# Weights' decode: VectorE's five operations with one tensor input get a column of constants as a second tensor input

## The chip, the core and the metric

The kernel runs on one core of one Trainium2 chip. The metric is the device time of one execution in microseconds (us); less is better. Before the change it is 2730.36 us, the median of three runs.

## What is computed

Three layers follow each other on 2 x 12480 tokens with 128 features: a long convolution with a filter that a small network makes of the positions, done by Fourier transforms and gated by x; a layer 128 to 2048 to 128 with a squared ReLU; and a layer 128 to 2048 to 128 with h cos(h).

```python
def _attn_ref(x, v, pos_emb, w1, w2):
    h_mlp = np.maximum(pos_emb @ w1, 0.0) @ w2
    h_filt = h_mlp * np.exp(-0.01 * pos)[:, None]
    u = x * v
    Uf = np.fft.rfft(u, n=2 * S, axis=1)
    Hf = np.fft.rfft(h_filt, n=2 * S, axis=0)
    y = np.fft.irfft(Uf * Hf[None], n=2 * S, axis=1)[:, :S]
    return x * y

def _moe_ref(x, w_in, w_out):
    h = x @ w_in
    r = np.maximum(h, 0.0)
    return (r * r) @ w_out

def _moe2_ref(x, w_in, w_out):
    h = x @ w_in
    return (h * np.cos(h)) @ w_out
```

The four weight matrices are drawn in double precision. The kernel gets their bits as pairs of 32-bit integers and splits each weight into a high and a low part, for matmuls in three terms.

## The kernel before

The work has three stages. The **first stage** takes the first transform of the convolution in 30 chunks of two pairs each (the loop over `n, (q, i)`). A pair multiplies x by v on GpSimd (L191), takes the filter's small network through TensorE and ScalarE (L182 to L198), runs eight matmul records into A (L212), copies one half to SBUF on ScalarE (L214) and adds and subtracts on VectorE into bt (L216), which is then stored to HBM. Loads of chunks come from the SP queue into five buffers, and a load is issued when TensorE has freed its buffer; bt has three buffers. The **second stage** (from about 230 us) takes the second transform, multiplies the spectra and goes back. The **third stage** (from about 470 us) runs the last transform and the two layers as one long loop of matmuls with operations of ScalarE, VectorE and GpSimd between them.

The change lies in the **decode of the weights**, the generator `weight(step)`. It has sixteen steps, one for each quarter of each matrix (four of sixteen row or column blocks, so 128 x 512 elements). A step reads `raw` in SBUF, whose pairs of integers give `lo` and `hi`, and works on the tiles w_a, w_b and w_r: VectorE masks the sign away (L102), takes the sign and sets a bit of it (L103), bounds the magnitude (L105), shifts the exponent into place (L107), puts sign and magnitude together (L108), takes the power of two alone (L110), and multiplies the low half by it (L113). ScalarE rounds to the high part wh (L112), and GpSimd makes the low part wl in two operations (L115, L117). All of these tiles lie in SBUF.

The generator is cut into seven pieces by its `yield`s. The first stage's loop takes two pieces behind each pair with `decode(2)`, from the third pair on, so that a step is spread over three and a half pairs and the sixteen steps over 56 of the 60. The order on each engine is the order in which the program issues: VectorE runs the decode's pieces between the bt of the pairs, and GpSimd runs L115 and L117 between the L191, which are issued four pairs ahead. Where L115 waits for L113, the L191 behind it wait as well.

Of the kernel before, what the change touches and what calls it, by code (L numbers as in the profile page):

```python
# [8 lines left out]
F32 = mybir.dt.float32  # L9
F32R = mybir.dt.float32r  # L10
I32 = mybir.dt.int32
U32 = mybir.dt.uint32
AF = mybir.ActivationFunctionType
ALU = mybir.AluOpType
# [43 lines left out]
def conv_moe(ctx, tc, t):  # L58
    nc = tc.nc
    cst = ctx.enter_context(tc.tile_pool(name="cst", bufs=1))  # L60
# [4 lines left out]
    nc.vector.memset(halfpi, HALF_PI)  # L65
    quarter = cst.tile([128, 1], F32, name="quarter")
    nc.vector.memset(quarter, -0.25)
    warm = cst.tile([128, 1], F32, name="warm")
    Gt = cst.tile([2 * HB, 2, 128], F32, name="Gt")
    It = cst.tile([128, 2, 2 * HB], F32, name="It")  # L70
# [10 lines left out]
    def raw_of(step):  # L81
        m, f0 = divmod(step, 4)
        f = slice(4 * f0, 4 * f0 + 4)
        raw = wt.tile([128, 4, 128, 2], I32, tag="wr", name="wr", bufs=2)
        src = t[("moe_w_in", "moe_w_out", "moe2_w_in", "moe2_w_out")[m]].bitcast(I32)
        src = src.rearrange("(f p) (e t) -> p f e t" if m % 2 else "p (f e t) -> p f e t", f=NF, t=2)
        nc.sync.dma_start(out=raw, in_=src[:, f])
        raws[step] = raw, W[1 + m // 2, m % 2], f

    def weight(step):  # L90
        if step not in raws:
            raw_of(step)
        n = WORDER.index(step) + 1
        if n < 16:
            raw_of(WORDER[n])
        raw, (wh, wl), f = raws.pop(step)
        lo, hi = raw.bitcast(U32)[:, :, :, 0], raw[:, :, :, 1]
        a, b, r = (wt.tile([128, 4, 128], I32, tag=f"w_{n}", name=f"w_{n}") for n in "abr")
        af, bf, rf = a.bitcast(F32), b.bitcast(F32), r.bitcast(F32)
        ts = nc.vector.tensor_scalar  # L100
        yield
        ts(out=a, in0=hi, scalar1=0x7fffffff, scalar2=None, op0=ALU.bitwise_and)  # L102
        ts(out=b, in0=hi, scalar1=-0x80000000, scalar2=0x40000000, op0=ALU.bitwise_and, op1=ALU.bitwise_xor)  # L103
        yield
        ts(out=af, in0=af, scalar1=2.0 ** -15, scalar2=122880.0, op0=ALU.max, op1=ALU.min)  # L105
        yield
        ts(out=a, in0=a, scalar1=4, scalar2=1, op0=ALU.logical_shift_left, op1=ALU.logical_shift_right)  # L107
        nc.vector.tensor_tensor(out=a, in0=a, in1=b, op=ALU.bitwise_xor)  # L108
        yield
        ts(out=b, in0=a, scalar1=-0x800000, scalar2=None, op0=ALU.bitwise_and)  # L110
        yield
        nc.scalar.activation(wh[:, f], af, AF.Copy)  # L112
        nc.vector.scalar_tensor_tensor(out=rf, in0=lo, scalar=2.0 ** -52, in1=bf, op0=ALU.mult, op1=ALU.mult)  # L113
        yield
        nc.gpsimd.tensor_tensor(out=bf, in0=af, in1=wh[:, f].bitcast(F32), op=ALU.subtract)  # L115
        yield
        nc.gpsimd.tensor_tensor(out=wl[:, f], in0=bf, in1=rf, op=ALU.add)  # L117

    steps = (x for k in WORDER for x in weight(k))

    def decode(n):
# [683 lines left out]
```

## Time and profile before

| | us |
|---|---|
| median of three runs | 2730.36 |
| lowest, highest | 2729.28, 2736.08 |
| the profiled execution | 2726.36 |
| its span, first to last instruction | 2724.3 |

The profiled execution is the one that the profile was taken of. Its rows are times from the span's start. PE is TensorE (PEld its weight loads), DVE VectorE, ACT ScalarE, POOL GpSimd, SP SyncE, whose queue issues most transfers; an engine's name with a q is its sequencer. L12 is line 12 of the kernel. An instruction's duration counts what it waits inside, once it has been started; what an engine waits for a semaphore before it stands apart, as idle time with the one that ended it.

### The profile page before, as it was taken

The page shows a single profiled execution, that of the slowest core. Times are in us where ns is not written, and L with a number is a line of the kernel's source. Part 1 is how long each engine was busy: PE and PEld are TensorE (multiplying, and loading weights), DVE is VectorE, ACT ScalarE, POOL GpSimd, SP SyncE. Part 2 cuts the span into 40 slices and gives each one's busy share as a digit, 9 for nine tenths or more (in the row PEclk, how much of TensorE's full clock was granted, in tenths as well). Part 3 has the DMA queues.
Part 4 walks back from the last instruction along what each step waited for, and adds up shares of the span by engine and source line. Part 5 has one row for each costly group of instructions (what it writes and reads, how often), then busy time and mean ns, then how long its engine had stood idle before and what let it go on. Part 6 is the DMA issues. An engine that isn't in the chain of part 4 may idle for free.

```text
span 2724.3 us, 38773 instructions
## 1 busy us (share of the span) xinstructions
PE 2681.8 (98%) x11762; PEld 2104.9 (77%) x11762; DVE 2402.7 (88%) x4675; ACT 2383.1 (87%) x4295; POOL 1353.2 (50%) x1050
## 2 busy tenths in 40 slices
PE   8998999999999999999999999999999999999999
PEld 5554444888888888888888888888888888888887
DVE  6997998888888888888888888888888888888888
ACT  4446997899999999999999999999999999999998
POOL 4565886244444444444444444444444444444455
PEclk9999999999999999999999999999999999999999
DMA  9997997110100110101110101111101111101000
GB/s 396 421 411 260 298 300 232 46 29 31 30 26 23 32 29 18 43 16 33 29 33 16 45 16 33 29 32 29 32 17 33 29 33 29 32 17 32 17 9 10
DMA packets 86771, 219.64 MB, mean 81 GB/s; under 512 B 6025, under 2 KB 49633, under 8 KB 82689
## 3 DMA queue, kind: packets, MB, share of 16 engines
q1 hardware_dynamic: 79298, 180.24, 20.1%
q10 hardware_dynamic: 7263, 36.92, 3.3%
q8 instruction: 93, 1.52, 0.2%
q14 instruction: 117, 0.96, 0.1%
HBM read 140.37 MB, written 77.07 MB: 80 GB/s over the span
## 4 chain that ended last, share of the span: by engine, by line
PE 81%; ACT 1%; DVE 1%; issue 0%; SPq 0%; POOLq 0%; POOL 0%; DMA 0%; DVEq 0%; ACTq 0%
PE h L565 13%; PE h L567 13%; PE y L581 13%; PE h L566 13%; PE y L579 13%; PE y L580 13%; PE pc L531 4%; DVE g L653 0%; ACT k L630 0%; DVE r L638 0%; ACT r L604 0%; DVE gh L663 0%; ACT g L610 0%; ACT c L645 0%; ACT gh L661 0%
## 5 line engine op out<-in xcount | busy, mean ns | idle before, releaser
L670 POOL TENSOR_TENSOR gl<-g,gh 128x512 fp32r<-128x512 f32 (+2 forms) x800 | 1040.8, 1301 | 1220.1 <-ACT gh L661 717.4
L653 DVE TENSOR_TENSOR g<-h,c 128x512 f32<-128x512 f32 (+2 forms) x800 | 538.6, 673 | 208.5 <-ACT c L645 197.4
L630 ACT ACTIVATE k<-h,quarter 128x512 int32<-128x512 f32 (+2 forms) x800 | 540.7, 676 | 121.5 <-PE h L567 117.4
L565 PE MATMUL h<-zh,wh 128*128 128x512 f32 (+2 forms) x1600 | 624.9, 391 | 1.2 <-DVE zh L549 0.9
L581 PE MATMUL y<-gl,wh 128*128 128x512 f32 (+2 forms) x1600 | 617.8, 386 | 4.1 <-POOL gl L670 2.2
L579 PE MATMUL y<-gh,wl 128*128 128x512 f32 (+2 forms) x1600 | 616.2, 385 | 0.7 <-DVE gh L617 0.7
L567 PE MATMUL h<-zh,wl 128*128 128x512 f32 (+2 forms) x1600 | 615.2, 384 | 0.0
L566 PE MATMUL h<-zl,wh 128*128 128x512 f32 (+2 forms) x1600 | 614.3, 384 | 0.0
L580 PE MATMUL y<-gh,wh 128*128 128x512 f32 (+2 forms) x1600 | 614.1, 384 | 0.0
L645 ACT ACTIVATE c<-r,halfpi 128x512 f32<-128x512 f32 (+2 forms) x800 | 565.4, 707 | 2.6 <-DVE r L638 2.6
L624 DVE TENSOR_TENSOR gl<-g,gh 128x512 fp32r<-128x512 f32 (+2 forms) x800 | 535.8, 670 | 1.1
L638 DVE CUSTOM_DVE_ANT_0 r<-h,k 128x512 f32<-128x512 f32 (+2 forms) x800 | 535.6, 669 | 0.0
L604 ACT ACTIVATE r<-h 128x512 f32<-128x512 f32 (+2 forms) x800 | 471.5, 589 | 69.2 <-PE h L567 57.0
L610 ACT ACTIVATE g<-r 128x512 f32<-128x512 f32 (+2 forms) x800 | 492.9, 616 | 1.0 <-DVE gl L624 0.4
L617 DVE CAST gh<-g 128x512 fp32r<-128x512 f32 (+2 forms) x800 | 331.9, 415 | 37.8 <-ACT g L610 34.9
L581 PEld LDWEIGHTS y<-gl,wh 128*128 128x128 f32 x1600 | 300.3, 188 | 70.3 <-POOL gl L670 7.7
L579 PEld LDWEIGHTS y<-gh,wl 128*128 128x128 f32 x1600 | 300.4, 188 | 61.2 <-DVE zl L592 1.2
L580 PEld LDWEIGHTS y<-gh,wh 128*128 128x128 f32 x1600 | 300.7, 188 | 59.6
L567 PEld LDWEIGHTS h<-zh,wl 128*128 128x128 f32 x1600 | 300.4, 188 | 59.7
L565 PEld LDWEIGHTS h<-zh,wh 128*128 128x128 f32 x1600 | 300.9, 188 | 56.9 <-issue 1.0
L566 PEld LDWEIGHTS h<-zl,wh 128*128 128x128 f32 x1600 | 300.7, 188 | 54.9
L661 ACT ACTIVATE gh<-g 128x512 fp32r<-128x512 f32 (+2 forms) x400 | 246.0, 615 | 0.1
(67 smaller groups left out, 2426.2 us busy)
## 6 DMA issues: line engine op xcount, KB each, us to landing
ld<-ld SPq DMA_DIRECT2D x30, 1336.0 KB
B<-Bs SPq DMA_DIRECT2D x25, 1536.0 KB
dt<-Ds SPq DMA_DIRECT2D x59, 416.0 KB
Ds<-dt SPq DMA_DIRECT2D x24, 960.0 KB
Bs<-bt ACTq DMA_DIRECT2D x28, 768.0 KB
Bs<-bt ACTq DMA_DIRECT2D x28, 480.0 KB
xt<-xT SPq DMA_DIRECT2D x60, 208.0 KB
out<-o SPq DMA_DIRECT2D x47, 256.0 KB
```

What stands on the lines that cost most here:

```text
L565: nc.tensor.matmul(h[:, :n], wh[:, f, :], zh[:, :n], start=True, stop=False)
L566: nc.tensor.matmul(h[:, :n], wh[:, f, :], zl[:, :n], start=False, stop=False)
L567: nc.tensor.matmul(h[:, :n], wl[:, f, :], zh[:, :n], start=False, stop=True)
L579: nc.tensor.matmul(y[:, :n], wl[:, f, :], gh[:, :n], start=a, stop=False)
L580: nc.tensor.matmul(y[:, :n], wh[:, f, :], gh[:, :n], start=False, stop=False)
L581: nc.tensor.matmul(y[:, :n], wh[:, f, :], gl[:, :n], start=False, stop=b)
L624: nc.vector.tensor_tensor(out=gl[:, :n], in0=g[:, :n], in1=gh[:, :n].bitcast(F32), op=ALU.subtract)
L630: nc.scalar.activation(k[:, :n], hp[2, u][:, :n], AF.Identity, scale=-1.0, bias=quarter)
L638: nc.vector._custom_dve(TENSOR_ADD_SAT, out=r[:, :n], in0=h[:, :n], in1=k[:, :n], s0=0.25, s1=-0.75)
L645: nc.scalar.activation(c[:, :n], r[:, :n], AF.Sin, bias=halfpi, scale=TWO_PI)
L653: nc.vector.tensor_tensor(out=g[:, :n], in0=h[:, :n], in1=c[:, :n], op=ALU.mult)
L670: nc.gpsimd.tensor_tensor(out=gl[:, :n], in0=g[:, :n], in1=gh[:, :n].bitcast(F32), op=ALU.subtract)
```

## The change

Five operations with one tensor input and scalars, `tensor_scalar`, become `scalar_tensor_tensor`: the first tensor with a scalar, and the result with a second tensor. The second tensor is a column of a new tile `consts` of four constants a partition, read at a step of zero for all 512 elements. Where the operation had no second scalar, one that leaves the value alone stands in (or with 0), and the mask of L102 becomes a shift to the left and back by one. Four small writes at the start fill `consts`. L108, L112, L113, L115 and L117 stay, as does the order of all.

```diff
+    consts = cst.tile([128, 4], I32, name="consts")
+    nc.vector.memset(consts[:, 0:1], 1)
+    nc.vector.memset(consts[:, 3:4], 0)
+    nc.vector.memset(consts[:, 1:2], 0x40000000)
+    nc.vector.memset(consts[:, 2:3].bitcast(F32), 122880.0)
...
-        ts = nc.vector.tensor_scalar
+        tt = nc.vector.scalar_tensor_tensor
+
+        def const(n):
+            return consts[:, n:n + 1].unsqueeze(2).to_broadcast([128, 4, 128])
+
         yield
-        ts(out=a, in0=hi, scalar1=0x7fffffff, scalar2=None, op0=ALU.bitwise_and)
-        ts(out=b, in0=hi, scalar1=-0x80000000, scalar2=0x40000000, op0=ALU.bitwise_and, op1=ALU.bitwise_xor)
+        tt(out=a, in0=hi, scalar=1, in1=const(0), op0=ALU.logical_shift_left, op1=ALU.logical_shift_right)
+        tt(out=b, in0=hi, scalar=-0x80000000, in1=const(1), op0=ALU.bitwise_and, op1=ALU.bitwise_xor)
         yield
-        ts(out=af, in0=af, scalar1=2.0 ** -15, scalar2=122880.0, op0=ALU.max, op1=ALU.min)
+        tt(out=af, in0=af, scalar=2.0 ** -15, in1=const(2).bitcast(F32), op0=ALU.max, op1=ALU.min)
         yield
-        ts(out=a, in0=a, scalar1=4, scalar2=1, op0=ALU.logical_shift_left, op1=ALU.logical_shift_right)
+        tt(out=a, in0=a, scalar=4, in1=const(0), op0=ALU.logical_shift_left, op1=ALU.logical_shift_right)
         nc.vector.tensor_tensor(out=a, in0=a, in1=b, op=ALU.bitwise_xor)
         yield
-        ts(out=b, in0=a, scalar1=-0x800000, scalar2=None, op0=ALU.bitwise_and)
+        tt(out=b, in0=a, scalar=-0x800000, in1=const(3), op0=ALU.bitwise_and, op1=ALU.bitwise_or)
         yield
```

## Rows read from the trace of the kernel before

**Rows 1.** The page's first part: each engine's busy us, share of the span, instructions.
```profile
PE 2681.8 (98%) x11762; PEld 2104.9 (77%) x11762; DVE 2402.7 (88%) x4675; ACT 2383.1 (87%) x4295; POOL 1353.2 (50%) x1050
```

**Rows 2.** Stretches: length, busy us of PE, PEld, DVE, ACT, POOL; clock, DMA share, GB/s.
```profile
20.00:40.00 20.00, 20.00 (x70) 12.76 (x69) 14.85 (x20) 10.93 (x23) 9.63 (x8) 1.00 1.02 402
40.00:200.00 160.00, 149.64 (x503) 91.28 (x502) 156.83 (x182) 77.13 (x173) 89.99 (x70) 1.00 1.02 418
200.00:226.00 26.00, 23.20 (x79) 13.99 (x78) 23.13 (x32) 10.91 (x24) 12.17 (x10) 1.00 0.77 281
230.00:480.00 250.00, 239.98 (x608) 108.27 (x608) 226.12 (x367) 224.04 (x386) 192.97 (x154) 0.99 0.85 273
480.00:2724.00 2244.00, 2236.84 (x10481) 1872.06 (x10479) 1979.54 (x4073) 2055.19 (x3681) 1040.77 (x800) 1.00 0.09 27
```

**Rows 3.** Waits from 40 to 200 us, DVE's and SP's: us, times, longest.
```profile
DVE bt L216 <- PE A L212: 1.3, 3, 0.4
DVE bt L216 <- issue: 0.8, 3, 0.3
...
SPq L165 <- PE A L212: 98.1, 22, 6.4
```

**Rows 4.** Groups by line, 0 to 420 us: shapes, count, busy us, mean ns, idle before.
```profile
L102 DVE TENSOR_SCALAR w_a<-wr 128x512 int32<-128x512 int32 x16 | 23.1, 1442 | 0.5 <-DMA wr<-moe_w_in 0.5
L103 DVE TENSOR_SCALAR w_b<-wr 128x512 int32<-128x512 int32 x16 | 21.7, 1358 | 0.0
...
L105 DVE TENSOR_SCALAR w_a<-w_a 128x512 f32<-128x512 f32 x16 | 17.1, 1067 | 0.0
...
L108 DVE TENSOR_TENSOR w_a<-w_a,w_b 128x512 int32<-128x512 int32 x16 | 11.1, 692 | 0.6
L113 DVE SCALAR_TENSOR_TENSOR w_r<-wr,w_b 128x512 f32<-128x512 uint32 x16 | 11.0, 687 | 0.3
...
L107 DVE TENSOR_SCALAR w_a<-w_a 128x512 int32<-128x512 int32 x16 | 6.7, 419 | 0.3
...
L65 DVE MEMSET halfpi<- 128x1 f32 x1 | 0.1, 59 | 0.8 <-PEq L792 0.8
```

**Rows 5.** Timeline of DVE in one step: start, us, line, operation.
```profile
123.35 2.53 DVE L102 TENSOR_SCALAR w_a<-wr 128x512 int32<-128x512 int32 x1
125.80 1.50 DVE L103 TENSOR_SCALAR w_b<-wr 128x512 int32<-128x512 int32 x1
...
128.95 0.98 DVE L105 TENSOR_SCALAR w_a<-w_a 128x512 f32<-128x512 f32 x1
```

**Rows 6.** Timeline of POOL in the same step.
```profile
121.87 1.27 POOL L115 TENSOR_TENSOR w_b<-w_a,wh 128x512 f32<-128x512 f32 x1 [6.04 <-DVE w_r L113]
123.10 1.27 POOL L191 TENSOR_TENSOR ut<-ld 104x512 f32<-104x512 f32 x1
124.33 1.26 POOL L117 TENSOR_TENSOR wl<-w_b,w_r 128x512 fp32r<-128x512 f32 x1
125.55 4.09 POOL L191 TENSOR_TENSOR ut<-ld 104x512 f32<-104x512 f32 x3
```

**Rows 7.** DVE's L381 beside POOL's L374: timeline, then ns min/median/max by line.
```profile
457.34 1.31 DVE L381 TENSOR_TENSOR y<-p,p 128x512 f32<-128x512 f32 x1
...
456.84 2.94 POOL L374 TENSOR_TENSOR p<-w,hi 128x512 f32<-128x512 f32 x2 [0.61 <-ACT w L356]
...
L381 DVE TENSOR_TENSOR y<-Z,p x26: 678/680/692, 239.9 to 455.0; 128x512 f32<-128x512 f32 x26
L381 DVE TENSOR_TENSOR y<-p,p x3: 686/693/1314, 457.3 to 460.4; 128x512 f32<-128x512 f32 x3
...
L374 POOL TENSOR_TENSOR p<-w,hi x79: 1262/1273/1716, 238.6 to 458.1; 128x512 f32<-128x512 f32 x79
```

**Rows 8.** Timeline at the handover to the second stage, SP and PE.
```profile
225.92 2.05 SPq L235 DMA_DIRECT2D B<-bt  x3
...
230.96 0.67 PE L320 MATMUL H<-B,Gt 120*128 120x512 f32 x1 [3.52 <-DMA B<-bt]
```

## The prediction

> **What bounds the kernel now.** I read the page's busy shares first: TensorE is busy 98% of the span, VectorE 88%, GpSimd 50% [rows 1]. These are averages over stages with different limits, and the operations that change all lie in the first stage, so the next view is busy time by stretch [rows 2]. From 480 us on TensorE is busy 2236.84 of 2244 us: there it sets the time, and whatever shifts its start shifts the end by as much. Between 40 and 200 us, in the stage that holds the decode, VectorE is busy 156.83 of 160 us, TensorE 149.64, GpSimd 89.99, and the DMA engines 1.02 of their time at 418 GB/s. So VectorE and DMA are both full there; which of them leads? The waits of that stretch answer it [rows 3]: VectorE's bt operations wait 1.3 us for TensorE and 0.8 us for nothing visible, and the queue that issues the loads waits 98.1 us for TensorE to free a buffer. Compute waits for no load, the loads wait for compute. VectorE sets the pace, and time added to it there goes to the end. DMA is so full that time taken from VectorE would soon meet a second limit.
>
> **What the five operations cost now.** The groups by line [rows 4] are the main view. Each of the sixteen decode steps has seven VectorE operations on 128x512 elements. L107, with one tensor input, takes 419 ns, and L110 is its like (one row stands for both). L108 and L113, with two, take 692 and 687 ns. L102, L103 and L105 have one tensor input as well, yet their means are 1442, 1358 and 1067 ns. The surplus over 420 ns is a wait inside the instruction, and the two timelines of one step show for whom [rows 5, 6]. L102 starts at 123.35 us and ends at 125.88. GpSimd's L191 runs from 123.10 to 124.37 and its L117 from 124.33 to 125.59: L102 ends 0.29 us after L117 does. L103 starts at 125.80 and ends at 127.30, in a stretch in which three L191 take 4.09 us. Three at 1.27, each starting 0.04 before the last one's end as L191 and L117 do, would take 3.73; the two that a VectorE operation goes ahead of are 0.18 longer, 1.45. L105 ends at 129.93, again 0.29 us after the last L191 (125.55 + 4.09 = 129.64). The four operations after it find GpSimd idle until L113 is done, for which L115 waits (6.04 us at 121.87), and keep to their length alone. So VectorE and GpSimd shut each other out for whole instructions, and both pay. Summed over the stage the waits are (1442 + 1358 + 1067 - 3 x 420) x 16 = 41.7 us of VectorE's time.
>
> **The change, part by part.** *Four constants written at the start:* 59 ns each by L65 [rows 4], 0.24 us in all, in a stretch in which VectorE has no input yet. It costs nothing; were that cover gone, 0.24 us.
>
> *L102, L103, L105, L107 and L110 become operations with two tensor inputs.* Their length alone goes from 420 to about 690 ns; the nearest rows are L113, of the same instruction kind, at 687 and L108, on integers, at 692 [rows 4]. The bounds are 0.42, nothing added, and 0.69; I take 0.69, as these two rows have the operands of the new form. That is +0.27 us each, 5 x 0.27 = 1.35 us a step, 16 x 1.35 = 21.6 us in all.
>
> *What of the 41.7 us of waits?* This decides the sign, and L108 and L113 don't tell, since GpSimd is idle when they run [rows 6]. The nearest rows are at the end of the second stage [rows 7]. L381 as y<-p,p has both inputs in SBUF. At 457.34 us it meets GpSimd's L374, which began at 456.84 and takes 1.27 us alone; L381 takes 1314 ns instead of 686 to 693, and of the two L374 the longer takes 1716 ns instead of 1273. As y<-Z,p, with Z in PSUM and one input in SBUF, the same line never takes more than 692 ns in 26 times, in a stage in which GpSimd is busy 192.97 of 250 us [rows 2]. So two inputs in SBUF don't escape GpSimd: L381 ends at 458.65, 0.54 us after the first L374 (458.11), where the one-input operations of the decode end 0.29 us after. The second L374 is held up by 0.44 us, where an L191 is held up by 0.18. On both engines the collision costs some 0.26 us more than now, the difference of the two lengths. All operands of the changed operations (raw halves, w_a, w_b, consts) lie in SBUF, so I take the collision as it is in [rows 7].
>
> One rule of the Trainium skill says the same and one can be read against it. SBUF — State Buffer, section Who interferes with whom, has a VectorE instruction with two SBUF inputs contend with a GpSimd instruction that reads SBUF; the row of L381 agrees with it. Advanced Engine Details and Errata, section Mode Summary, names only the 2-port modes of VectorE as what GpSimd blocks, by which the new operations would be free of it; that is the second rival's mechanism, and the row of L381 speaks against it.
>
> *Does a step keep its waits?* I follow the step of [rows 5, 6]. L102 starts as now, waits for L117's end at 125.59 and ends 0.55 later, at 126.14 (+0.26). The first L191 starts that much later, L103 waits for it and ends at +0.53, the second L191 is pushed by 0.53 too, and so is the third; L105 starts at +0.53, still waits for the third, and ends at +0.80. L107 and L110 meet no one: +1.07 and +1.34. VectorE's delays are GpSimd's delays, so each wait stays. L113, for which the next burst of GpSimd waits, comes 1.34 us later, and the next step finds the same order of things.
>
> *What lies on the path.* The first step runs before 40 us, where VectorE is busy only 14.85 of 20 us [rows 2]; its 1.34 us are covered by that. Fifteen steps remain: 15 x 1.34 = 20.1 us. VectorE's idle time in front of bt between 40 and 200 us, 1.3 + 0.8 = 2.1 us [rows 3], is a lag of TensorE, which would be ahead when VectorE is later: -2.1. The last step still counts, since the last bt come behind it and the second stage's first matmul waits for DMAs that are issued after them (225.92, 230.96 [rows 8]). That handover may shorten a little, because DMA, full at 418 GB/s now, gets 20.1 us more for the same bytes, and part of what keeps it busy until 226 us would be done earlier: I estimate -1 of the 5 us between those two rows, with bounds 0 and -2.5. The sum is 20.1 - 2.1 - 1 = +17.0 us. Behind it nothing changes: the second stage and TensorE's stretch from 480 us on are shifted as a whole.
>
> The profiled execution took 2726.36 us (span 2724.3), 4.0 us under the median of the runs, 2730.36. So the profiled one would become 2743.4, and the median 2730.36 + 17.0 = **2747.4 us**, 0.6% slower. A measurement of this kernel can tell about 0.3%, 8.2 us, from no change.
>
> **Rivals.** (1) *The waits shrink as the operations grow.* If GpSimd's burst were not pushed back, L105 would fall behind its end. Its wait, (1067 - 420) x 16 = 10.4 us [rows 4], would go: +17.0 - 10.4 = +6.6, 2737 us, within 0.3%. For it: L105 meets only the last 0.7 us of a burst in the step shown. Against it: a longer VectorE operation holds GpSimd as well ([rows 7], 1716 ns), so the burst moves along. (2) *The other side: two-input operations aren't held up by GpSimd.* Then all five take 690 ns flat, and VectorE saves (1442 + 1358 + 1067 + 2 x 419 - 5 x 690) x 16 = 20.1 us. It could not all be had: DMA has no free time before 200 us, and of 200 to 226 us 23% of 26, 6.0 us [rows 2]. So -6, 2724 us: within 0.3% of the median by the centre, and faster by over 0.3% only if DMA can give more than its 418 GB/s, up to the full 20.1 us and 2710. It decides at the first collision: L102 has to end while a GpSimd operation runs. For it: operations with an input in PSUM pass GpSimd unharmed (L381 at 692 ns at most); against it: the one that matches in operands doesn't. (3) *More rounds are lost.* L102 lost one in the step shown: it was waiting when L191 ended, and L117 went first. If in every second step one more operation loses a round of 1.27 us [rows 6], 7 x 1.27 = 8.9 us come on top: 2756 us. (4) *The change is none:* the chip runs the new form as fast as the old, 2730 us. L113, of that form, at 687 ns speaks against it.
>
> **How the numbers follow.** Forecast 75%; rival 3, 12%; rival 1, 5%; rival 2, 6%, split evenly between within and faster; rival 4, 2%. Slower by over 0.3% (above 2738.6): 0.75 + 0.12 = 0.87 and half of rival 1's spread, some 0.02, so 0.89; within 0.3%: 0.08; faster: 0.03. The range for 8 in 10: downwards the forecast less a wait of half of L105 (5.2 us), the handover's bound (1.5) and the gaps of [rows 3] counted twice (2.1), 2738.6; upwards to rival 3, 2756. I take 2738.5 to 2757.
>
> **What would show it.** Means near L102 1.71, L103 1.63, L105 1.33, L107 and L110 0.69 us; the longest of GpSimd's L191 near 1.72 us instead of 1.45; the last bt near 244 instead of 226 us, VectorE still near 98% busy up to it, DMA near 0.93 rather than 1.02 there. From TensorE's first matmul of the second stage on, stretches as long as now. The forecast is wrong if L102 and L103 take 0.69 us while GpSimd runs (rival 2: then bt waits for DMA), if L105 sinks to 0.69 (rival 1), or if L102's mean passes 2 us (rival 3).

## The result, and the profile after

The changed kernel takes 2749.97 us (median of six runs, 2747.27 to 2754.64), the kernel before in its six 2731.25. The ratio is 1.0072, with a 95% interval of 1.0062 to 1.0082: slower by 16.9 to 22.4 us. The profiled execution took 2748.93 us, with a span of 2746.8.

The groups by line answer to [rows 4]. Line numbers are 9 higher here (L111, L112, L114, L116 and L119 are the five); behind the bar stand busy us and the mean of one in ns.

```profile
L111 DVE SCALAR_TENSOR_TENSOR w_a<-wr,consts 128x512 int32<-128x512 int32 x16 | 28.6, 1786 | 0.1
L112 DVE SCALAR_TENSOR_TENSOR w_b<-wr,consts 128x512 int32<-128x512 int32 x16 | 26.0, 1622 | 0.0
L114 DVE SCALAR_TENSOR_TENSOR w_a<-w_a,consts 128x512 f32<-128x512 f32 x16 | 20.3, 1272 | 0.0
...
L119 DVE SCALAR_TENSOR_TENSOR w_b<-w_a,consts 128x512 int32<-128x512 int32 x16 | 11.0, 686 | 0.3
...
L116 DVE SCALAR_TENSOR_TENSOR w_a<-w_a,consts 128x512 int32<-128x512 int32 x16 | 10.9, 684 | 0.3
```

The two operations that meet no GpSimd instruction went from 420 to 685 ns, the length alone of a two-input operation. The other three grew by 344, 264 and 205 ns. Together the five means add up to 6050 ns instead of 4708 (1442 + 1358 + 1067 + 419 + 422): 1.34 us a step, 21.5 us in all. The waits inside the three, (1786 + 1622 + 1272 - 3 x 685) x 16 = 42.0 us, are what they were, 41.7.

The same step as in [rows 5, 6], VectorE's timeline first (start, us, line), then GpSimd's:

```profile
133.87 2.80 DVE L111 SCALAR_TENSOR_TENSOR w_a<-wr,consts 128x512 int32<-128x512 int32 x1
136.59 1.75 DVE L112 SCALAR_TENSOR_TENSOR w_b<-wr,consts 128x512 int32<-128x512 int32 x1
...
140.00 1.25 DVE L114 SCALAR_TENSOR_TENSOR w_a<-w_a,consts 128x512 f32<-128x512 f32 x1
...
134.85 1.27 POOL L126 TENSOR_TENSOR wl<-w_b,w_r 128x512 fp32r<-128x512 f32 x1
136.08 4.62 POOL L200 TENSOR_TENSOR ut<-ld 104x512 f32<-104x512 f32 x3
```

L111 outwaits L126 (to 136.12) and ends 0.55 us behind it, where the old form ended 0.29 behind. The three L200 take 4.62 us instead of 4.09: GpSimd is held up by 0.26 us more at each of the two collisions. That step begins at 133.87 us instead of 123.35, 10.5 us later. One L200 alone (min/median/max in ns; L191 took 1462 at most) and the handover to the second stage, answering to [rows 8]:

```profile
L200 POOL TENSOR_TENSOR ut<-ld x60: 1257/1294/1782, 7.7 to 232.6; 104x512 f32<-104x512 f32 x60
...
247.95 1.98 SPq L244 DMA_DIRECT2D B<-bt  x3
...
251.69 1.78 PE L329 MATMUL H<-B,Gt 120*128 120x512 f32 x3 [2.82 <-DMA B<-bt]
```

The last bt, two operations, in the kernel before and in the changed one:

```profile
225.29 1.02 DVE L216 TENSOR_TENSOR bt<-A,v 128x384 f32<-128x384 f32 x2 [2.28 <-ACT v L214]
```

```profile
246.25 1.02 DVE L225 TENSOR_TENSOR bt<-A,v 128x384 f32<-128x384 f32 x2 [1.80 <-ACT v L223]
```

VectorE starts the last bt at 246.25 us instead of 225.29 (+21.0), SP begins to issue the DMAs from them at 247.95 instead of 225.92 (+22.0), and the second stage's first matmul starts at 251.69 instead of 230.96 (+20.7). From there to the end of the span it is 2495.1 us against 2493.3. So the loss is the first stage's. The 1.8 us further on are less than what this part differs by between the traces of all runs, whose instructions are the same there (2493.3 to 2499.3 us). By stretch (length, busy us of PE, PEld, DVE, ACT, POOL, granted clock, DMA share, GB/s), beside [rows 2]:

```profile
40.00:200.00 160.00, 139.58 (x448) 82.98 (x447) 156.19 (x163) 67.94 (x155) 87.28 (x63) 0.97 1.00 379
250.00:500.00 250.00, 240.59 (x582) 108.60 (x583) 223.66 (x359) 221.86 (x380) 192.88 (x154) 0.97 0.85 272
500.00:2746.00 2246.00, 2239.27 (x10506) 1874.71 (x10504) 1981.55 (x4081) 2056.55 (x3687) 1041.03 (x800) 1.00 0.10 27
```

VectorE is as busy as before, TensorE 10 us less, and DMA moves 379 GB/s instead of 418: the first stage runs at VectorE's pace, which is slower.

### The profile page after: what moved, and what is told of

Its sections match the earlier page's. It is cut to its first block, busy times and chain, and to the rows that moved or that the text cites. A ratio compares the mean times of both kernels' runs of the same rounds, so it can differ in the third digit from the quotient of the medians.

```text
span 2746.8 us, 38778 instructions
## 1 busy us (share of the span) xinstructions
PE 2692.5 (98%) x11762; PEld 2109.9 (77%) x11762; DVE 2423.7 (88%) x4679; ACT 2381.0 (87%) x4295; POOL 1360.4 (50%) x1050
## 4 chain that ended last, share of the span: by engine, by line
PE 80%; DVE 1%; ACT 1%; issue 0%; POOLq 0%; DVEq 0%; ACTq 0%
PE h L574 13%; PE h L576 13%; PE h L575 13%; PE y L590 13%; PE y L588 13%; PE y L589 13%; PE pc L540 4%; DVE g L662 0%; DVE r L647 0%; ACT k L639 0%; DVE gh L672 0%; ACT g L619 0%; ACT c L654 0%; ACT r L613 0%; ACT gh L670 0%
```

## The experiments

The kernel before took 2730.66 us beside runs 1 to 4, and the ratios are against it. Two questions: does the loss add up from length and unchanged waits, and what makes the waits (runs 1 to 4)? And what would VectorE's time have been worth in the other direction, as the second rival priced it (runs 5 to 7)?

**1. The two operations that collide with nothing.** The changed kernel with L102, L103 and L105 in their old form:

```diff
 (against the changed kernel)
-        tt(out=a, in0=hi, scalar=1, in1=const(0), op0=ALU.logical_shift_left, op1=ALU.logical_shift_right)
+        ts(out=a, in0=hi, scalar1=0x7fffffff, scalar2=None, op0=ALU.bitwise_and)
...
```

> Only L107 and L110 get the column of constants, the two operations that meet no GpSimd instruction. Theory (length and kept waits add up): 2 x 0.27 us a step, 15 steps on the path, +8.1 us to 2739 us; means 0.69 us for these two, and the means of the other three as before (1.44, 1.36, 1.07 us). Rival (the added time comes from the collisions alone): within 2 us of 2731. Rival (DMA paces the stage): within 2 us of 2731, with VectorE idle longer before bt.

Measured: 2738.6 us, ratio 1.0026 (1.0016 to 1.0035), +4.4 to +9.6 us. The groups by line:

```profile
L112 DVE TENSOR_SCALAR w_a<-wr 128x512 int32<-128x512 int32 x16 | 24.0, 1499 | 2.4 <-DMA wr<-moe_w_in 2.4
L113 DVE TENSOR_SCALAR w_b<-wr 128x512 int32<-128x512 int32 x16 | 22.8, 1428 | 0.0
L115 DVE TENSOR_SCALAR w_a<-w_a 128x512 f32<-128x512 f32 x16 | 17.2, 1073 | 0.0
...
L120 DVE SCALAR_TENSOR_TENSOR w_b<-w_a,consts 128x512 int32<-128x512 int32 x16 | 11.0, 687 | 0.3
...
L117 DVE SCALAR_TENSOR_TENSOR w_a<-w_a,consts 128x512 int32<-128x512 int32 x16 | 10.9, 684 | 0.3
```

The second stage's first matmul, 230.96 us in the kernel before:

```profile
239.57 1.96 PE L330 MATMUL H<-B,Gt 120*128 120x512 f32 x4 [0.82 <-DMA B<-bt]
```

That is +8.6 us. The length of two operations that nothing holds up costs what it adds. That the loss comes from collisions alone is out, and so is that DMA paces the stage. The waits of the three, untouched here, stay too: (1499 + 1428 + 1073 - 3 x 420) x 16 = 43.8 us.

**2. The three that collide.** The other half: only L102, L103 and L105 in the new form.

```diff
 (against the changed kernel)
-        tt(out=a, in0=a, scalar=4, in1=const(0), op0=ALU.logical_shift_left, op1=ALU.logical_shift_right)
+        ts(out=a, in0=a, scalar1=4, scalar2=1, op0=ALU.logical_shift_left, op1=ALU.logical_shift_right)
...
-        tt(out=b, in0=a, scalar=-0x800000, in1=const(3), op0=ALU.bitwise_and, op1=ALU.bitwise_or)
+        ts(out=b, in0=a, scalar1=-0x800000, scalar2=None, op0=ALU.bitwise_and)
```

> Only the three operations that collide with GpSimd (mask, sign, bounds) get the column of constants. Theory: 3 x 0.27 us a step, 15 steps, +12.1 us to 2743 us; their means 1.71, 1.63, 1.34 us, waits of 41.7 us in all as before; L107 and L110 at 0.42. Rival (waits shrink as operations grow): under +6 us, means that add up to less than 4.2 us. Rival (more rounds lost): over +18 us.

Measured: 2744.13 us, ratio 1.0042 (1.0027 to 1.0057), +7.4 to +15.6 us.

```profile
L112 DVE SCALAR_TENSOR_TENSOR w_a<-wr,consts 128x512 int32<-128x512 int32 x16 | 27.7, 1729 | 0.3 <-DMA wr<-moe_w_in 0.3
L113 DVE SCALAR_TENSOR_TENSOR w_b<-wr,consts 128x512 int32<-128x512 int32 x16 | 25.9, 1620 | 0.0
L115 DVE SCALAR_TENSOR_TENSOR w_a<-w_a,consts 128x512 f32<-128x512 f32 x16 | 20.3, 1266 | 0.0
```

And the second stage's first matmul:

```profile
243.03 3.51 PE L330 MATMUL H<-B,Gt 120*128 120x512 f32 x4 [2.49 <-DMA B<-bt]
```

The waits are (1729 + 1620 + 1266 - 3 x 685) x 16 = 41.0 us. They neither shrink (the means add up to 4.6, not under 4.2) nor multiply. The two halves, some +7.1 and +11.5 us by their ratios, add up to 18.6, the whole change's +19.7 within the intervals. In the traces the first stage shows it with less scatter: the second stage's first matmul comes 8.6 us later in run 1 and 12.1 in run 2, and the whole change moves it by 20.7.

**3 and 4. The same operations with the constants in PSUM.** All banks are taken in the first stage, so one buffer of its small PSUM tile goes; run 3 is the kernel before with that alone, run 4 is the change with its constants there.

```diff
 (run 3, against the kernel before; in run 4 too)
-        psM = st.enter_context(tc.tile_pool(name="psM", bufs=2, space=PSUM))
+        psM = st.enter_context(tc.tile_pool(name="psM", bufs=1, space=PSUM))
 (run 4, against the changed kernel)
-    consts = cst.tile([128, 4], I32, name="consts")
...
+        psC = st.enter_context(tc.tile_pool(name="psC", bufs=1, space=PSUM))
+        consts = psC.tile([128, 4], I32, name="consts")
...
```

> The kernel before with one buffer instead of two for the small PSUM tile of the first stage, which frees a bank: the base for the next kernel. Theory: TensorE is ahead of VectorE in that stage, so 0 to +5 us. Rival: the filter's small network now stalls TensorE at each pair, +15 us and more.

> The change with its constants in the freed PSUM bank instead of SBUF, so each of the five operations has one input in SBUF and one in PSUM; beside one_bank. Theory (GpSimd holds up an operation with two SBUF inputs, and not one with an input in PSUM): all five means at 0.69 us, GpSimd's L191 never over 1.30 us, 20.1 us less of VectorE's time than in one_bank, of which DMA, full at 418 GB/s, lets through about 6: one_bank - 6 us. Rival (DMA is not a limit): one_bank - 15 to - 20 us. Rival (a second tensor input is what collides, wherever it lies): one_bank + 18 us, means as in the changed kernel.

Measured: one buffer less, 2735.4 us, ratio 1.0014 (1.0004 to 1.0024); the constants in PSUM, 2735.65 us, ratio 1.0018 (1.0007 to 1.0028). Of run 4, the three operations by line, and GpSimd's x times v (min/median/max in ns):

```profile
L108 DVE SCALAR_TENSOR_TENSOR w_b<-wr,consts 128x512 int32<-128x512 int32 x16 | 10.9, 684 | 6.4 <-POOL wl L122 6.4
...
L107 DVE SCALAR_TENSOR_TENSOR w_a<-wr,consts 128x512 int32<-128x512 int32 x16 | 10.9, 679 | 3.9 <-DMA wr<-moe_w_out 3.9
L110 DVE SCALAR_TENSOR_TENSOR w_a<-w_a,consts 128x512 f32<-128x512 f32 x16 | 10.9, 679 | 0.0
...
L202 POOL TENSOR_TENSOR ut<-ld x60: 1262/1273/1290, 7.7 to 215.1; 104x512 f32<-104x512 f32 x60
```

These are the clearest rows of the study. The operations are those of the changed kernel; only the place of a tile of four columns differs, and the one buffer that makes room for it. In SBUF the three take 1786, 1622 and 1272 ns and GpSimd's L200 up to 1782; in PSUM they take 679 to 684, and GpSimd never more than 1290. It is not that they no longer meet. L107 here lies within GpSimd's L202 and keeps its length:

```profile
128.08 0.68 DVE L107 SCALAR_TENSOR_TENSOR w_a<-wr,consts 128x512 int32<-128x512 int32 x1
...
127.83 1.28 POOL L202 TENSOR_TENSOR ut<-ld 104x512 f32<-104x512 f32 x1
```

In this form of the operation the collision belongs to the second input in SBUF. The old forms, with one input, collide as well [rows 4, 5]. (The 6.4 us before L108 are a wait for GpSimd to be done with the tile, outside the instruction.)

The time did not follow. Between 40 and 200 us, run 3 and then run 4:

```profile
40.00:200.00 160.00, 149.72 (x494) 89.36 (x493) 148.22 (x180) 77.69 (x171) 88.46 (x69) 1.00 1.02 408
```

```profile
40.00:200.00 160.00, 149.80 (x498) 90.15 (x496) 137.28 (x181) 78.93 (x170) 85.24 (x70) 1.00 1.01 409
```

VectorE is busy 11 us less in the same stretch, and TensorE and DMA do the same work. What TensorE waits for there (us, times, longest), in run 3 and in run 4:

```profile
PE hp L196 <- ACT hT L184: 9.5, 22, 0.4
```

```profile
PE hp L207 <- ACT hT L195: 9.5, 22, 0.4
```

With one buffer gone, the filter's network makes TensorE wait for ScalarE 22 times, about once in each chunk, 9.5 us in all. Busy 149.72 us and waiting 9.5, it has less than 1 us of 160 left: in both runs TensorE paces the stage, and VectorE (148.22 busy) doesn't. So the expected -6 us failed, and this pair doesn't say what VectorE's time was worth in the kernel before.

**5 to 7. Less of VectorE's work, less of DMA's, and both.**

```diff
 (run 5: fewer loads)
...
+        if WORDER.index(step) > 1:
+            raws[step] = kept[WORDER.index(step) % 2], W[1 + m // 2, m % 2], f
+            return
...
 (run 6: no bounds)
-        ts(out=af, in0=af, scalar1=2.0 ** -15, scalar2=122880.0, op0=ALU.max, op1=ALU.min)
 (run 7: both)
```

> The kernel before, leaving out fourteen of the sixteen loads of raw weights (all steps decode the first two blocks, so the weights are not the reference's): 7.3 of some 83 MB of the first stage, 17.6 us of DMA at 418 GB/s, with VectorE's work untouched. Theory (VectorE paces the stage in the kernel before): 0 to -3 us, what the handover gains, the last bt within 2 us of 226. Rival (DMA paces it and VectorE's full share is coincidence): -10 to -17 us.

> The kernel before, leaving out the bounds of L105 in each step (magnitudes are not bounded): 17.1 us less of VectorE's time, waits on GpSimd among it. Theory of the prediction (DMA lets through about 6 us of what VectorE saves): -4 to -8 us, about 2725, with bt waiting for its stores or TensorE for loads. Rival (VectorE's time is worth its full length in both directions): -13 to -17 us, about 2716. Rival (the wait moves to the next operation): under -3 us, with L107 near 1 us.

> Both edits together, leaving out the bounds and fourteen of the sixteen loads. Theory (DMA is the next limit behind VectorE): the gain is larger than that of the bounds alone by 4 us or more, -10 to -15 us, up to where TensorE, busy 149.6 of 160 us before, sets the pace. Rival (DMA never was the next limit, TensorE is): the same as without the bounds alone, within 2 us.

Measured, against 2730.2 us for the kernel before beside them:

| | us | ratio | interval |
|---|---|---|---|
| 5: fewer loads | 2731.07 | 1.0000 | 0.9992 to 1.0009 |
| 6: no bounds | 2732.6 | 1.0009 | 1.0000 to 1.0017 |
| 7: both | 2725.35 | 0.9980 | 0.9971 to 0.9989 |

Run 5 agrees with VectorE's pace: 7.3 MB less to move bring nothing, and the last bt start at 226.25 us. Run 6 is a miss: the theory's 4 to 8 us do not come, and there is no gain at all. VectorE even has more than 17.1 us less to do. L102 and L103 shrink to 1105 and 1088 ns in their means, and of the wait that the last rival moves to the next operation only 0.21 us a step arrive there (631 ns instead of 419):

```profile
L106 DVE TENSOR_SCALAR w_a<-w_a 128x512 int32<-128x512 int32 x16 | 10.1, 631 | 0.0
```

(1442 + 1358 + 1067 + 419 + 422 - 1105 - 1088 - 631 - 422) x 16 = 23.4 us of VectorE's time are gone. Run 7 answers in part: each edit alone brings nothing, both together 0.2%. The stretches from 40 to 200 us of runs 5, 6 and 7:

```profile
40.00:200.00 160.00, 149.72 (x502) 91.16 (x501) 156.31 (x182) 76.60 (x172) 89.69 (x70) 1.00 0.99 375
```

```profile
40.00:200.00 160.00, 146.76 (x481) 89.83 (x480) 133.90 (x164) 73.95 (x165) 85.89 (x67) 0.97 1.01 411
```

```profile
40.00:200.00 160.00, 152.11 (x511) 94.33 (x510) 144.39 (x171) 78.81 (x175) 91.47 (x72) 0.99 0.99 381
```

Without the bounds VectorE is idle 26 us of 160, and most of what it waits for is new; the waits of run 6 between 40 and 200 us (us, times, longest), then of run 7:

```profile
DVE w_a L102 <- DMA wr<-moe_w_out: 8.4, 3, 4.8
...
DVE bt L215 <- PE A L211: 5.8, 8, 1.8
...
DVE bt L215 <- DMA Bs<-bt: 2.7, 3, 1.5
```

```profile
DVE bt L219 <- DMA Bs<-bt: 7.3, 6, 2.8
...
DVE bt L219 <- PE A L215: 5.4, 8, 1.7
```

In run 6 raw weights arrive late and stores are not out in time, neither of which VectorE waited for from 40 us on before [rows 3]. (Another 4.4 us of L102 are put down to GpSimd, and 3.7 us of bt to ScalarE's copy.) The trace of run 6 is that of its slowest execution, 2736.58 us, with the second stage's first matmul at 236.18 us, so its waits may be longer than those of the median. With fewer loads the weights come in time, and what is left is the stores and TensorE, busy 152.11 of 160 us. So DMA, and TensorE close behind it, stand right behind VectorE. Run 7 gave less than the expected 10 to 15 us; how its remaining limit divides between stores and TensorE was not tested. Nor do these runs part the bytes from the queue: the raw loads share SP's queue with the loads of chunks, and in run 6 it stands 26.5 us before a raw load until VectorE has freed the buffer. Run 7 takes both away.

## Why the prediction was right

It forecast 2747.4 us, 17.0 more; measured were 2749.97, and 19.7 more by the ratio. By its steps:

- **VectorE paces the first stage** [rows 2, 3]: shown. Runs 1 and 2 charge added time in full (+8.6 and +12.1 us at the handover, 8.1 and 12.1 expected), run 5 finds no gain in lighter DMA.
- **The length, 0.27 us each**: 684 and 686 ns measured for the two alone, against 419 and 422.
- **The collision stays, because both inputs lie in SBUF** [rows 7]: shown by run 4, where it disappears with the constants' place. A single L381 of 1314 ns in another stage carried this step. It gave the right sizes: 0.55 us behind GpSimd's end instead of 0.29, L200 up to 1782 ns where 1.72 us was forecast. The Trainium skill's SBUF — State Buffer, Who interferes with whom, agrees with these rows; the reading of Advanced Engine Details and Errata, Mode Summary, by which only the 2-port modes collide, doesn't.
- **Each wait is kept, since GpSimd is pushed along**: 41.7 us before, 42.0 after, and the step at 133.87 us runs as it was followed by hand, 2.80, 1.75 and 1.25 us. That the next step finds the same order of things was wrong, though: the steps are of two kinds. L102 takes 2.53 us in seven of the sixteen, every second one from the third on, and 0.42 to 0.58 in eight others. The working followed one kind only; that the waits of the other are kept too is what the sum of the means shows.
- **The first step is covered**: mostly. The second step's first operation starts at 39.49 us instead of 39.16, so 1.0 of the first step's 1.34 us was hidden.
- **VectorE's 2.1 us of idle time would go**: wrong. Its idle time between 40 and 200 us is 160 - 156.19 = 3.8 us, 3.2 before. A later VectorE makes TensorE wait longer for it to free A, 12.0 us instead of 4.1, and bt then waits no more for TensorE but for ScalarE's copy v, which is made behind TensorE's matmuls:

```profile
PE A L221 <- DVE bt L225: 12.0, 11, 1.8
...
DVE bt L225 <- ACT v L223: 2.8, 4, 1.6
```

- **The handover gives 1 us back**: by the two rows of [rows 8] it seems so, 251.69 - 247.95 = 3.7 instead of 5.0 us. But those DMAs do not start the handover: they are issued 1.7 us after the last bt's start instead of 0.6, for a reason that no run tested. From the last bt's start to the matmul it is 5.4 us instead of 5.7, so 0.2 come back.

The last bt come 21.0 us later, against 18.0 forecast; 2.1 of the 3.0 us that lack are the idle time and 0.3 the first step. The second step grew by more than 1.34 us: the third one's first operation moved from 48.57 to 50.87 us, 2.3 in place of 1.7. From there to 133.87 us six steps brought 8.2 us, 1.37 each, and the rest up to the last bt 10.4 us, eight steps of 1.30, about as forecast. So the mechanism held and the small terms did not: the two that were to give time back, 3.1 us together, gave 0.2.

Rivals 1, 3 and 4 left no sign: L114's mean is 1272 ns and not 690, L111's 1786 and not over 2000, and the two operations without a collision take 685 ns and not 420.

**The second rival's price was wrong, though its mechanism was rightly rejected.** I let it have 6 us because DMA had idle time behind 200 us [rows 2]. Run 6, the nearest case, took 23.4 us from VectorE and got nothing: its loads and stores came late before 200 us, and DMA's idle time behind that didn't help. TensorE, which the price left out, would have been a limit as well: it is busy 149.64 of the 160 us [rows 2], so of 20.1 us less on VectorE at most some 12 could have been had in that stage (an estimate: from 39 to 226 us are 187 us, times the 10.4 of 160 us that TensorE is idle). I had also read the DMA share of 1.02 as a measure of how full DMA is, and forecast 0.93 after the change. It is 1.00 after, at 379 GB/s, and 0.99 in run 5 at 375. The share stays near 1 while DMA moves a tenth less. The gigabytes a second, and who waits for DMA, tell more.

## What to carry to other kernels

A column of constants as a second tensor input is not free on VectorE: the operation takes its two-input length, 685 instead of 420 ns here, and with both inputs in SBUF it is still shut out by GpSimd for whole instructions, as [rows 7] showed before the change; with the constants in PSUM it isn't, and GpSimd isn't held up either. Where an engine is 98% busy in a stage and the others wait for it, added time is charged nearly in full, but that says nothing about removed time: here 23 us less brought nothing, since DMA and TensorE were nearly as full. Look for a colliding pair of the new kind somewhere in the trace before reckoning with a wait that will go.

## What the runs showed of the hardware

That TensorE's granted clock would dip was not expected. It is 0.97 between 40 and 200 us after the change and 1.00 before, with TensorE busy 139.58 instead of 149.64 of 160 us; VectorE sets the pace there, and no row tells what the dip costs. At the handover to the third stage it is 0.74 in the changed kernel:

```profile
480.00:500.00 20.00, 17.86 (x70) 12.56 (x71) 12.85 (x32) 6.29 (x16) 1.31 (x1) 0.74 0.59 178
```

About half of these 20 us went at 1.2 instead of 2.4 GHz. The kernel before has 0.99 from 230 to 480 us and 1.00 behind [rows 2]. Whether this makes the 1.8 us behind the handover to the second stage is open. It can't be all that makes this part longer or shorter: in run 2's trace the same stretch went at the full clock,

```profile
480.00:500.00 20.00, 16.05 (x105) 13.03 (x104) 13.40 (x40) 8.90 (x25) 0.00 (x0) 1.00 0.57 166
```

and from its handover to the end it is 2741.7 - 243.03 = 2498.7 us, longer than in the kernel before and in the changed one.
